# Seven products in every tile and an inverse DFT stage split by parity, in a fused spectral-filter and GELU kernel

## The chip, the cores and the metric

The kernel runs on one core of a Trainium2 chip. The metric is the device time of one launch in microseconds; the kernel before takes 768.41 us, the median of 9 runs (767.4 to 769.58).

## What is computed

```python
X = np.fft.rfft(x, axis=1)                        # x: (8, 3008, 256)
y = np.fft.irfft(X * (filt_r + 1j * filt_i), n=3008, axis=1)
h = y.reshape(24064, 256) @ w_in                  # w_in: (256, 2048)
g = 0.5 * h * (1 + erf(h / sqrt(2)))
out = g @ w_out                                   # w_out: (2048, 256)
```

Each of the 8 batches is filtered along its 3008 rows, and then 24,064 rows go through a two-layer MLP with an exact GELU. Inputs and output are float32; the products run in bfloat16 and float16.

## The kernel before, in words

**The filter.** 3008 is 47 x 64, so the transform is done as products with small matrices. `s1` (L291) is the DFT over the 47 rows that lie 64 apart; its products have 64 output rows and 47 input rows, so they use a quarter of TensorE each. Its result goes to DRAM (`R1`) and comes back as `b_sb` through `r1` (L314), turned so that the other index lies on the partitions. `s2` (L321) is the DFT over 64, for two frequencies k a step (12 steps a batch), with its twiddles in the table T2, one matrix for each of 24 k. It then multiplies by the filter: real and imaginary parts are swapped by two copies on ACT (L332, L333), and DVE takes two products and a sum (L334 to L336). `s3` (L340) is the inverse over 64, with one matrix of T3 for each k; its result goes to DRAM (`R2`) and comes back as `d_sb` through `r2` (L360). `s4` (L369) is the inverse over 47, with one small matrix T4 for all columns, and writes the filtered rows into a ring (`y_sb`) that holds two batches. The copies out of PSUM in s1, s3 and s4 are all made by DVE (`_evac`, L273).

Batch 0 has stages of its own (`c1` to `c4`), which transpose on TensorE instead of going through DRAM. Its `c2` (L409) multiplies by the filter in one DVE operation on 1024 columns (L420) and leaves the sum to the products of `c3`, with two matrices each. The filters are loaded into partitions 0 to 63 and copied to 64 to 127 (`dup_filters`, L97).

**The MLP.** The 24,064 rows are 47 tiles of 512. `mm1` (L482) makes one block of 128 hidden columns a call with two products of 512 columns (L490), and ACT's GELU takes it out of PSUM (L493). `mm2` (L495) is the second product: per slot four products of 256 columns (L517), with two copies and two stores a tile. `mm2_seven` (L563) is the same with seven half-size products instead of eight (Strassen-Winograd): per slot seven products of 128 columns (L578). It needs sums of the activations on DVE (`sums_1` to `sums_3`, L541 to L561: eight operations of 128x1024 a tile), eight DVE combinations (L591 to L601), and sums of the second weights, which POOL makes once (`weight_sums`, L527). It is used in 25 of the 47 tiles: the odd ones from 1 to 39, and 41 to 45.

**The order.** The order of every engine's instructions is the order in which the program calls them. It is written out by hand: time is cut into slots, 16 to a tile. In slot 16 t + jc the program calls what `put` has entered there, then the second product of tile t - 1, part jc, then the first product of tile t, part jc (L774 to L781). The stages of a later batch b are entered before the slot `hi` in which its first tile starts (L746 to L763): s1 from hi - 94, r1 at hi - 80, s2 from hi - 69 every 3.5 slots, each s3 four slots after its s2, r2 at hi - 24, s4 in the last 17. From slot 82 on one batch's stages begin every 96 slots. Batch 1 has its own numbers. Loads of x, of filters and of weights stand on POOL's queue; the loads of the batch after next wait there for an s2 result through a one-element copy (`gate`, L102). All other transfers, the stores of the output among them, stand on SP's queue in the order of the calls.

**Buffers.** PSUM has three banks for mm1 ("h"), two for mm2 ("o") and three for the stages ("f"); each s1 borrows one h bank. In SBUF `pa`, `pb`, `pp`, `pv` and `pd` hold the results of s1, r1, s2, s3 and r2.

Of the kernel before, what the change touches and what calls it, by code (L numbers as in the profile page):

```python
# [19 lines left out]
K1 = 24  # L20
# [10 lines left out]
class _Mix:  # L31
    def __init__(self, ctx, tc, x, filt_r, filt_i, w_in, w_out, out):
        self.tc, self.nc = tc, tc.nc
        self.x, self.filt_r, self.filt_i = x, filt_r, filt_i
        self.w_in, self.w_out, self.out = w_in, w_out, out
        self.B, self.S, self.D = x.shape
        self.DFF = w_in.shape[1]
        assert self.S == NA * NB and self.D == 256 and self.DFF == 2048
        pool = lambda name, bufs, **kw: ctx.enter_context(tc.tile_pool(name=name, bufs=bufs, **kw))
        P = bass.MemoryType.PSUM  # L40
        self.const = pool("const", 1)
        self.px = pool("px", 1)
        self.pa = pool("pa", 3)
        self.pb = pool("pb", 4)
        self.pp = pool("pp", 4)
        self.pv = pool("pv", 3)
        self.pd = pool("pd", 3)
        self.pool = pool
        self.po = pool("po", 4)
        self.py = pool("py", 1)  # L50
        self.pg = pool("pg", 2)
        self.pq = pool("pq", 1)
        self.small = pool("small", 1)
        self.dram = pool("dram", 2, space=bass.MemoryType.DRAM)
        c = self.const
        self.T1 = c.tile([2 * NA, 96], BF16, name="T1")
        self.T2 = c.tile([128, K1, 2, NB], BF16, name="T2")
        self.T3 = c.tile([128, K1, 2, NB], BF16, name="T3")
        self.T4 = c.tile([96, NA, 2], BF16, name="T4")
        self.T4c = c.tile([96, NA, 2], BF16, name="T4c")  # L60
        self.F = c.tile([128, 2, K1, 256], BF16, name="F")
        self.w_in_sb = c.tile([128, 2, self.DFF], BF16, name="w_in_sb")
        self.w_out_sb = c.tile([128, 16, self.D], FP16, name="w_out_sb")
        self.w_sums = c.tile([128, 4, 8, 128], FP16, name="w_sums")
        self.ps, self.st = {}, {}
        self.flip = 0
# [29 lines left out]

    def dup_filters(self, eng, k0, k):  # L97
        for k in range(k0, k0 + k, 2):
            o, i = (self.F[r:r + 64, :, k:k + 2, :].rearrange("p t a b -> p t (a b)") for r in (64, 0))
            (eng.copy if eng is self.nc.scalar else eng.tensor_copy)(out=o, in_=i)  # L100
# [6 lines left out]
    def load_next(self, b, p, c, h):  # L107

        self.gate(self.st[b, "p", p][0:1, 0:1])
        self.load_x(b + 1, 8 * c, 8, (h,))  # L110
# [93 lines left out]
    def weights_4(self, g):  # L204

        ts = self.nc.gpsimd.tensor_scalar
        q, self.wt = (g.tile([128, 1], FP32, name=n) for n in ("q48", "wt"))
        ts(out=q, in0=self.p, scalar1=48.0, scalar2=-48.0, op0=ALU.is_ge, op1=ALU.mult)
        self.nc.gpsimd.tensor_tensor(out=q, in0=self.p, in1=q, op=ALU.add)
        ts(out=self.wt, in0=q, scalar1=2.0, scalar2=1.0, op0=ALU.is_ge, op1=ALU.add)  # L210
# [79 lines left out]

    def s1(self, b, c):  # L291
# [13 lines left out]
        for i in range(2):  # L305
            for h in range(2):
                self._evac(a[:, h, 2 * i:2 * i + 2, :].rearrange("p a b -> p (a b)"), ps[i][h], False)
# [13 lines left out]
    def s2(self, b, p):  # L321
        nc = self.nc
        ps = self.bank("ps_s2")
        for i in range(2):
            k = 2 * p + i
            nc.tensor.matmul(ps[:, 256 * i:256 * i + 256], lhsT=self.T2[:, k].rearrange("p a b -> p (a b)"),  # L326
                             rhs=self.st[b, "b", k // 6][:, k % 6, :], start=True, stop=True)

        w = self.pp.tile([128, 2, 512], BF16, tag="p12", name="p12")
        p1, p2 = w[:, 0], w[:, 1]  # L330
        f = lambda t: self.F[:, t, 2 * p:2 * p + 2, :].rearrange("p a b -> p (a b)")
        nc.scalar.activation(out=p2[0:64], in_=ps[64:128], func=AF.Copy, scale=-1.0)  # L332
        nc.scalar.copy(out=p2[64:128], in_=ps[0:64])  # L333
        nc.vector.tensor_tensor(out=p1, in0=ps, in1=f(0), op=ALU.mult)  # L334
        nc.vector.tensor_tensor(out=p2, in0=p2, in1=f(1), op=ALU.mult)
        nc.vector.tensor_tensor(out=p1, in0=p1, in1=p2, op=ALU.add)  # L336
        self.st[b, "p", p] = p1


    def s3(self, b, p):  # L340
        nc = self.nc
        if p == 0:
            self.st[b, "R2"] = self.dram.tile([48, NB, 256], BF16, tag="R2", name="R2")
        if p % 2 == 0:
            self.st[b, "v"] = self.pv.tile([128, 4, 256], BF16, tag="v", name="v_sb")
        vt, R2 = self.st[b, "v"], self.st[b, "R2"]
        ps = self.bank("ps_s3")
        w = self.st.pop((b, "p", p))
        for i in range(2):
            k = 2 * p + i  # L350
            nc.tensor.matmul(ps[:, 256 * i:256 * i + 256], lhsT=self.T3[:, k].rearrange("p a b -> p (a b)"),  # L351
                             rhs=w[:, 256 * i:256 * i + 256], start=True, stop=True)
        i = (p % 2) * 2
        self._evac(vt[:, i:i + 2, :].rearrange("p a b -> p (a b)"), ps, False)
        if p % 2 == 1:
            k = 2 * (p - 1)
            o = R2.rearrange("(k r) n c -> (r n) k c", r=2)
            nc.sync.dma_start(out=o[:, k:k + 4, :], in_=vt)

    def r2(self, b, c):  # L360
        d = self.pd.tile([96, 8, 256], BF16, tag="d", name="d_sb")
        self.st[b, "d", c] = d
        R2 = self.st[b, "R2"]
        for g in range(2):
            n = g * HB + c * 8
            self.nc.sync.dma_start(out=d[g * 48:g * 48 + 48, :, :], in_=R2[:, n:n + 8, :])


    def s4(self, b, grp, half):  # L369
# [4 lines left out]
        t4 = self.T4.rearrange("p a b -> p (a b)")  # L374
        for i in range(4):
            nc.tensor.matmul(ps[:, 94 * i:94 * i + 94],  # L376
                             lhsT=d[:, (grp % 2) * 4 + i, 128 * half:128 * half + 128],
                             rhs=t4, start=True, stop=True)
        yv = self.ring[:, half, o:o + self.S].rearrange("c (m w) -> c m w", w=HB)[:, :, 4 * grp:4 * grp + 4]
        pv = ps[:, 0:376].rearrange("c (i m) -> c m i", i=4)  # L380
        self._evac(yv, pv, False, 1.0 / self.S)
# [233 lines left out]
def kernel(  # L615
# [29 lines left out]
    cols = m.iota(g, "cols", [128, 128], [[1, 128]])  # L645
# [11 lines left out]
    m.T3i = m.pg.tile([128, K1, 2, NB], BF16, tag="g", name="T3i")  # L657
# [6 lines left out]
    m.dup_filters(nc.gpsimd, 4, 20)  # L664
# [54 lines left out]
    m.T1p = g.tile([2 * NA, 2, K1, 2], BF16, name="T1p")  # L719
    nc.gpsimd.tensor_copy(out=m.T1p, in_=m.T1.rearrange("p (h r k) -> p h k r", h=2, r=2))  # L720
    m.table_1_tiles(g)
    m.load_x(1)
    m.load_w_out(0)
    m.load_w_out(8)
    m.weights_4(g)
# [20 lines left out]
    for b in range(1, B):  # L746
        hi = first(b)
        if b == 1:
            s1, n1, r1, s2, n2, r2, s4, n4 = 0, 4, 15, 25, 2.8, 61, 68, 0.72
        else:  # L750
            s1, n1, r1, s2, n2, r2, s4, n4 = hi - 94, 3.5, hi - 80, hi - 69, 3.5, hi - 24, hi - 17, 1
        for u in range(16):
            put(s4 + int(u * n4), m.s4, b, u // 2, u % 2)
        for c in range(4):
            put(s1 + int(c * n1), m.s1, b, c)
            put(r1, m.r1, b, c)
            put(r2, m.r2, b, c)
        for p in range(12):
            put(s2 + int(n2 * p), m.s2, b, p)
            put(s2 + int(n2 * p) + 4, m.s3, b, p)  # L760
        if b + 1 < B:
            for i in range(8):
                put(s2 + int(n2 * (i + 2)), m.load_next, b, i + 2, i // 2, i % 2)  # L763

    put(20, m.table_4, m.T4, m.T1p, m.wt, "f", "act")
    put(6, m.weight_sums)
    seven = [t for t in range(1, NT - 1) if t % 2 or t > 40]
# [45 lines left out]
```

## Time and profile before

| | before |
|---|---|
| median of 9 runs (lowest, highest) | 768.41 us (767.4, 769.58) |
| the profiled execution, and its span | 768.41 us, 766.6 us |
| TensorE clock granted | 1.00 |
| GELU on ACT (L493), busy | 438.5 us, 752 of 597 ns |
| s2's copies on ACT (L332, L333), busy | 98.4 us, 168 of about 585 ns |
| DVE copies of s1, s3, s4 (L278, L280), mean | 684, 685, 545 ns |
| DVE sums for the seven products (L548, L554, L561), mean | 684, 687, 683 ns |
| first mm1 of the first tile starts | 38.9 us |
| first mm2 of the first tile starts | 50.3 us |

The span runs from the first to the last instruction; 1.8 us of the profiled execution lie around it. In a line of the timeline stand the start in us, the length, the engine, the source line and operation, what it writes and reads, its size and how many are drawn together. Matmuls are pipelined: each is listed with about 0.17 us of latency, so that what one costs is read from its start to the next one's start. DVE operations of one queue overlap by about 0.08 us in the same way.

### The profile page before, as it was taken

The page shows a single profiled execution, that of the slowest core. Times are in us where ns is not written, and L with a number is a line of the kernel's source. Part 1 is how long each engine was busy: PE and PEld are TensorE (multiplying, and loading weights), DVE is VectorE, ACT ScalarE, POOL GpSimd, SP SyncE. Part 2 cuts the span into 40 slices and gives each one's busy share as a digit, 9 for nine tenths or more (in the row PEclk, how much of TensorE's full clock was granted, in tenths as well). Part 3 has the DMA queues.
Part 4 walks back from the last instruction along what each step waited for, and adds up shares of the span by engine and source line. Part 5 has one row for each costly group of instructions (what it writes and reads, how often), then busy time and mean ns, then how long its engine had stood idle before and what let it go on. Part 6 is the DMA issues. An engine that isn't in the chain of part 4 may idle for free.

```text
span 766.6 us, 17716 instructions
## 1 busy us (share of the span) xinstructions
PE 742.5 (97%) x7136; PEld 525.8 (69%) x7257; DVE 551.6 (72%) x1085; ACT 568.5 (74%) x978; POOL 77.9 (10%) x173
## 2 busy tenths in 40 slices
PE   7998999999999999999999999999999999999998
PEld 4846775767777677676677767667677766777776
DVE  8958887586786868768677696767967679636562
ACT  7878966888668875698756986569865798667773
POOL 7851100020000200002000120001100000000000
PEclk9999999999999999999999999999999999999999
DMA  9884644456253662635526455254552422411011
GB/s 145 147 179 116 142 124 126 139 113 146 71 141 117 120 152 63 174 89 112 143 76 179 94 99 152 68 168 100 115 144 79 144 69 84 124 42 43 29 56 57
DMA packets 87283, 85.85 MB, mean 112 GB/s; under 512 B 6688, under 2 KB 77472, under 8 KB 87200
## 3 DMA queue, kind: packets, MB, share of 16 engines
q1 hardware_dynamic: 78816, 68.70, 31.2%
q0 software_dynamic: 8384, 16.00, 14.5%
q8 instruction: 57, 0.93, 0.5%
q14 instruction: 26, 0.21, 0.1%
HBM read 54.00 MB, written 46.66 MB: 131 GB/s over the span
## 4 chain that ended last, share of the span: by engine, by line
PE 86%; DVE 6%; ACT 3%; DMA 2%; issue 2%; POOL 0%; DVEq 0%; POOLq 0%; SPq 0%
PE ps_h L490 36%; PE ps_o L517 20%; PE ps_o L578 19%; PE ps_s L376 3%; PE ps_s L351 2%; PE ps_s L326 2%; PE ps_s L303 2%; ACT g_sb L493 2%; DVE s_sb L548 1%; DVE p L334 1%; DMA R<-a_sb 1%; ACT p L332 1%; PE ps_c L438 1%; DMA x_sb<-in_x_dram 1%; DMA F<-in_filt_i_dram 1%
## 5 line engine op out<-in xcount | busy, mean ns | idle before, releaser
L493 ACT ACTIVATE g_sb<-ps_h 128x512 f16<-128x512 f32 x752 | 438.5, 597 | 177.8 <-PE ps_h L490 148.7
L490 PE MATMUL ps_h<-y_sb,w_in_sb 128*128 128x512 bf16 (+3 forms) x1483 | 420.9, 365 | 1.7 <-DVE a_sb L278 1.6
L517 PE MATMUL ps_o<-w_out_sb,g_sb 128*128 128x256 f16 x1392 | 207.3, 273 | 1.6
L517 PEld LDWEIGHTS <-g_sb 128*128 128x128 f16 x1392 | 132.9, 98 | 70.4 <-issue 9.9
L490 PEld LDWEIGHTS <-w_in_sb 128*128 128x128 bf16 x1600 | 138.1, 98 | 15.7 <-issue 2.5
L578 PEld LDWEIGHTS <-g_sb 128*128 128x128 f16 x1600 | 106.0, 98 | 43.7 <-DVE g_sb L554 6.9
L334 DVE TENSOR_TENSOR p<-ps_s,F 128x512 bf16<-128x512 f32 x84 | 57.9, 689 | 63.4 <-ACT p L333 29.6
L578 PEld LDWEIGHTS <-s_sb 128*128 128x128 f16 x1200 | 81.5, 98 | 21.4
L278 DVE CAST a_sb<-ps_s 128x512 bf16<-128x512 f32 x112 | 69.5, 684 | 28.4 <-PE ps_s L303 26.1
L280 DVE TENSOR_SCALAR y_sb<-ps_s 128x376 bf16<-128x376 f32 x112 | 58.9, 545 | 38.1 <-PE ps_s L376 37.6
L578 PE MATMUL ps_o<-w_sums,g_sb 128*128 128x128 f16 x800 | 70.5, 219 | 4.5 <-DVE g_sb L554 3.8
L578 PE MATMUL ps_o<-w_out_sb,g_sb 128*128 128x128 f16 x800 | 66.3, 219 | 3.9 <-DVE ost L523 3.2
L578 PE MATMUL ps_o<-w_sums,s_sb 128*128 128x128 f16 x800 | 69.2, 219 | 0.7
L548 DVE TENSOR_TENSOR s_sb<-g_sb 128x1024 f16<-128x1024 f16 x100 | 65.5, 684 | 2.6 <-ACT g_sb L493 2.6
L105 POOL COPY gate<-p 1x1 bf16<-1x1 bf16 x48 | 13.9, 289 | 446.5 <-DVE p L336 446.5
L278 DVE CAST v_sb<-ps_s 128x512 bf16<-128x512 f32 x84 | 57.4, 685 | 0.9 <-PE ps_s L351 0.8
L332 ACT ACTIVATE p<-ps_s 64x512 bf16<-64x512 f32 x84 | 49.9, 594 | 2.1
L333 ACT CAST p<-ps_s 64x512 bf16<-64x512 f32 x84 | 48.5, 577 | 1.0
L523 DVE COPY ost<-ps_o 128x512 f32<-128x512 f32 x43 | 29.6, 687 | 26.8 <-PE ps_o L517 26.8
L376 PEld LDWEIGHTS <-d_sb 96*128 96x128 bf16 x448 | 30.8, 97 | 25.3 <-DMA d_sb<-R 0.2
L336 DVE TENSOR_TENSOR p<-p 128x512 bf16<-128x512 bf16 x84 | 35.7, 425 | 2.9
L376 PE MATMUL ps_s<-T,d_sb 96*128 96x94 bf16 x448 | 36.3, 204 | 1.4
(131 smaller groups left out, 550.8 us busy)
## 6 DMA issues: line engine op xcount, KB each, us to landing
out_dram<-ost SPq DMA_DIRECT2D x93, 256.0 KB, 2.4
x_sb<-in_x_dram POOLq DMA_DIRECT2D x64, 188.0 KB, 3.6
R<-a_sb SPq DMA_DIRECT2D x112, 96.0 KB, 2.1
b_sb<-R SPq DMA_DIRECT2D x28, 384.0 KB, 4.6
R<-v_sb SPq DMA_DIRECT2D x42, 256.0 KB, 2.5
d_sb<-R SPq DMA_DIRECT2D x56, 192.0 KB, 4.0
w_in_sb<-in_moe_w_in_dram POOLq DMA_DIRECT2D x2, 512.0 KB, 9.9
w_out_sb<-in_moe_w_out_dram POOLq DMA_DIRECT2D x2, 512.0 KB, 12.4
```

The lines of the kernel that those rows point to most:

```text
L278: self.nc.vector.tensor_copy(out=out, in_=in_)
L280: self.nc.vector.tensor_scalar(out=out, in0=in_, scalar1=scale, scalar2=None, op0=ALU.mult)
L332: nc.scalar.activation(out=p2[0:64], in_=ps[64:128], func=AF.Copy, scale=-1.0)
L333: nc.scalar.copy(out=p2[64:128], in_=ps[0:64])
L334: nc.vector.tensor_tensor(out=p1, in0=ps, in1=f(0), op=ALU.mult)
L336: nc.vector.tensor_tensor(out=p1, in0=p1, in1=p2, op=ALU.add)
L376: nc.tensor.matmul(ps[:, 94 * i:94 * i + 94], lhsT=d[:, (grp % 2) * 4 + i, 128 * half:128 * half + 128], rhs=t4, start=True, stop=True)
L490: nc.tensor.matmul(ps[:, o:o + n], lhsT=self.w_in_sb[:, dc, jc * 128:jc * 128 + 128], rhs=self.ring[:, dc, off:off + n], start=(dc == 0), ...
L493: nc.scalar.activation(out=self.st["g", t][:, jc, :], in_=ps, func=AF.Gelu)
L517: nc.tensor.matmul(ps[:, tile_i % 2, :], lhsT=g[:, jc, tile_i * 128:tile_i * 128 + 128], rhs=self.w_out_sb[:, jc, :], start=(jc == 0), sto ...
L548: self.nc.vector.tensor_tensor(out=self.st["s", t][:, i:i + 2], in0=a, in1=b, op=ALU.subtract)
L578: nc.tensor.matmul(ps[:, (m + 1) % 2, sub, :], lhsT=a[:, i, 128 * sub:128 * sub + 128], rhs=b[:, i], start=i == 0, stop=i == 7)
```

## The change

All of it is in one edit:

- `mm2_seven` is used for tiles 1 to 45 (45 instead of 25).
- s2 ends in one DVE operation that makes both products of the spectrum, with the real and with the imaginary filter, as c2 does; the two ACT copies and the sum go.
- s3 handles eight frequencies a call (four s2 steps). The rows of the spectrum are ordered by parity, so that one 64x64 matrix pair `U` serves all k; each call is 16 products of 64 input rows, 64 output rows and 512 columns into four PSUM banks, one of them an h bank. What differs between the k moves into s4, whose table `T4a` has its own 96x94 matrix for each of 32 columns. There are three calls a batch; half of the result is taken out by `s3_out` a slot later.
- The copies of s1, s3 and s4 are shared between DVE and ACT.
- The tables T2p (T2 in the new order), U and T4a are built at the start of the first batch's work: by POOL copies and products, three products and a few copies on TensorE and ACT, and 24 POOL operations for T4a.
- The filters must be in the new order for batches 1 to 7: they are written to DRAM once and read back, k 0 to 7 before the first slot and the rest at slot 16, on SP's queue.
- The second weights are loaded between the filter copies on POOL, ahead of the last six and of the x of batch 1.
- In the slots: s2 comes in groups of four (14 slots a group, 12 in batch 1) with s3 three slots after the fourth; the last r1 and the last r2 of a batch come later than the others; batch 1 loads the next x at slot 25 without gates.
- `pb`, `pp` and `pv` have 3, 6 and 2 buffers instead of 4, 4 and 3.

```diff
+    def save_filters(self):
+        self.Fd = self.dram.tile([64, 2, K1, 256], BF16, tag="Fd", name="Fd")
+        self.nc.sync.dma_start(out=self.Fd, in_=self.F[0:64])
+
+    def load_filters_again(self, k0, k):
+        for par in range(2):
+            for r in range(2):
+                for q in range(2):
+                    o = 64 * par + 32 * r + 16 * q
+                    self.nc.sync.dma_start(out=self.F[o:o + 16, :, k0:k0 + k, :],
+                                           in_=self.Fd[32 * q + (par ^ q):32 * q + 32:2, :, k0:k0 + k, :])
...
+    def table_4_all(self, g):
+        tt = self.nc.gpsimd.tensor_tensor
+        a, b = (self.t4[:, o:o + 8 * NA].rearrange("p (w m) -> p w m", w=8) for o in (224, 608))
+        to = self.T4a.rearrange("p w (m h) -> p h w m", h=2)
+        for w in range(0, HB, 8):
+            for h in range(2):
+                n = HB * h + w
+                for o, x in ((a, 0), (b, 1)):
+                    tt(out=o, in0=self.fcs[:, n:n + 8, x:x + 1].to_broadcast([96, 8, NA]),
+                       in1=self.G[:, x].unsqueeze(1).to_broadcast([96, 8, NA]), op=ALU.mult)
+                tt(out=to[:, h, w:w + 8], in0=a, in1=b, op=ALU.add)
...
     def s1(self, b, c):
-                self._evac(a[:, h, 2 * i:2 * i + 2, :].rearrange("p a b -> p (a b)"), ps[i][h], False)
+                self._evac(a[:, h, 2 * i:2 * i + 2, :].rearrange("p a b -> p (a b)"), ps[i][h], "act" if h else False)
...
     def s2(self, b, p):
-        nc.scalar.activation(out=p2[0:64], in_=ps[64:128], func=AF.Copy, scale=-1.0)
-        nc.scalar.copy(out=p2[64:128], in_=ps[0:64])
-        nc.vector.tensor_tensor(out=p1, in0=ps, in1=f(0), op=ALU.mult)
-        nc.vector.tensor_tensor(out=p2, in0=p2, in1=f(1), op=ALU.mult)
-        nc.vector.tensor_tensor(out=p1, in0=p1, in1=p2, op=ALU.add)
+        w = self.st[b, "p", p] = self.pp.tile([128, 2, 512], BF16, tag="p12", name="p12")
+        nc.vector.tensor_tensor(out=w, in0=ps.unsqueeze(1).to_broadcast([128, 2, 512]),
+                                in1=self.F[:, :, 2 * p:2 * p + 2, :].rearrange("p t a b -> p t (a b)"), op=ALU.mult)
...
+    def s3(self, b, u):
+        ps = [[self.bank("ps_s3", "h" if i == par == 0 else "f") for par in range(2)] for i in range(2)]
         for i in range(2):
+            for t in range(2):
+                for q in range(2):
+                    for par in range(2):
+                        r = slice(64 * par, 64 * par + 64)
+                        nc.tensor.matmul(ps[i][par][64 * q:64 * q + 64, :],
+                                         lhsT=self.U[r, t].rearrange("p r w -> p (r w)"),
+                                         rhs=self.st[b, "p", 4 * u + 2 * i + q][r, t, :], start=t == 0, stop=t == 1)
+        self.st[b, "ps3"] = ps
+        self.s3_out(b, u, 0)
+
+    def s3_out(self, b, u, i):
+        for par in range(2):
+            self._evac(vt[:, 2 * par:2 * par + 2, :].rearrange("p a b -> p (a b)"), ps[par], "act" if par else False)
+        for q in range(2):
+            self.nc.sync.dma_start(out=self.st[b, "R2"][:, 4 * u + 2 * i + q], in_=vt[64 * q:64 * q + 64])
...
     def s4(self, b, grp, half):
-                             rhs=t4, start=True, stop=True)
+                             rhs=self.T4a[:, 4 * grp + i], start=True, stop=True)
-        self._evac(yv, pv, False, 1.0 / self.S)
+        self._evac(yv, pv, "act" if half else False, 1.0 / self.S)
...
-    m.dup_filters(nc.gpsimd, 4, 20)
+    m.dup_filters(nc.gpsimd, 4, 8)
+    m.load_w_out(0)
+    m.load_w_out(8)
+    m.dup_filters(nc.gpsimd, 12, 12)
+    m.save_filters()
...
-            s1, n1, r1, s2, n2, r2, s4, n4 = 0, 4, 15, 25, 2.8, 61, 68, 0.72
+            s1, n1, r1, s2, n2, group, r2, s4, n4 = 0, 4, 15, 25, 2.5, 12, 62, 68, 0.72
-            s1, n1, r1, s2, n2, r2, s4, n4 = hi - 94, 3.5, hi - 80, hi - 69, 3.5, hi - 24, hi - 17, 1
+            s1, n1, r1, s2, n2, group, r2, s4, n4 = hi - 94, 3.7, hi - 80, hi - 71, 3.4, 14, hi - 25, hi - 17, 1
+        unit = lambda p: s2 + group * (p // 4) + int(n2 * (p % 4))
...
+            put(unit(p), m.s2, b, p)
+            if p % 4 == 3:
+                put(unit(p) + 3, m.s3, b, p // 4)
+                put(unit(p) + 4, m.s3_out, b, p // 4, 1)
...
-    seven = [t for t in range(1, NT - 1) if t % 2 or t > 40]
+    seven = range(1, NT - 1)
```

## Prediction

> **What bounds the kernel now.** I read the page's busy times first, then one period of a batch, then the stretch in it where PE waits. The profiled execution has a span of 766.6 us and took 768.41 us, which is also the median of the nine runs, so every sum below starts from 768.4.
>
> ```profile
> PE 742.5 (97%) x7136; PEld 525.8 (69%) x7257; DVE 551.6 (72%) x1085; ACT 568.5 (74%) x978; POOL 77.9 (10%) x173
> ...
> PE 86%; DVE 6%; ACT 3%; DMA 2%; issue 2%; POOL 0%; DVEq 0%; POOLq 0%; SPq 0%
> ```
>
> PE is the bound: 97% busy and 86% of the chain that ended last. Time comes only from fewer PE cycles or fewer PE waits. The timeline gives the two kinds of slot, one mm1 (two products of 512 columns) and one mm2 slot:
>
> ```profile
> 439.78 0.59 PE L490 MATMUL ps_h<-y_sb,w_in_sb 128*128 128x512 bf16 x2
> 440.21 0.60 PE L517 MATMUL ps_o<-w_out_sb,g_sb 128*128 128x256 f16 x4
> 440.65 0.59 PE L490 MATMUL ps_h<-y_sb,w_in_sb 128*128 128x512 bf16 x2
> ...
> 695.77 0.59 PE L490 MATMUL ps_h<-y_sb,w_in_sb 128*128 128x512 bf16 x2
> 696.20 0.55 PE L578 MATMUL ps_o<-w_sums,s_sb 128*128 128x128 f16 x7
> 696.59 0.59 PE L490 MATMUL ps_h<-y_sb,w_in_sb 128*128 128x512 bf16 x2
> ```
>
> From start to start a plain slot takes 0.87 us (440.65 - 439.78) and a seven-product slot 0.82 (six in a row: 692.91 to 697.85, 0.823 each). I use 0.046 us as the gain of a converted slot. The next lines, from the table of stretches and the timeline, are one batch period (96 slots, six tiles), its worst stretch, and the block of s1:
>
> ```profile
> 210.69:304.27 93.58, 91.83 (x882) 65.58 (x900) 69.14 (x134) 70.07 (x121) 6.29 (x16) 1.00 0.49 119
> 254.60:268.20 13.60, 12.43 (x123) 8.53 (x125) 12.96 (x26) 11.33 (x21) 3.56 (x8) 1.00 0.51 102
> ...
> 303.67 0.59 PE L490 MATMUL ps_h<-y_sb,w_in_sb 128*128 128x512 bf16 x2
> 304.20 0.63 PE L303 MATMUL ps_s<-x_sb,T1s 47*64 47x512 bf16 x8
> 304.75 0.61 PE L517 MATMUL ps_o<-w_out_sb,g_sb 128*128 128x256 f16 x4
> ```
>
> Columns of the first two: length, then PE, PEld, DVE, ACT, POOL busy. In 254.6 to 268.2 a seven-product tile meets s2 and s3: DVE is busy 12.96 of 13.60 us and PE only 12.43. The gaps between neighbouring matmuls beyond their usual spacing add up to 1.9 us a batch, all of them there (0.66 at 260.7, 0.47 at 257.0, then smaller), so a batch is 91.7 us of work and 1.9 of waiting. The s1 block costs 0.55 us plus 0.10 by which the mm1 before it is stretched (0.53 instead of 0.43): 0.65 us for eight 64-column products of 512 columns. One after the other they would take 8 x 0.216 = 1.7, so four run at a time.
>
> [...] 0.65 less two groups at 0.216 leaves 0.22 us for entering and leaving. [...] The trace shows one direction:
>
> ```profile
> 441.48 0.69 DVE L548 TENSOR_TENSOR s_sb<-g_sb 128x1024 f16<-128x1024 f16 x1
> ...
> 441.69 0.51 POOL L105 COPY gate<-p 1x1 bf16<-1x1 bf16 x1 [2.10 <-DVE p L336]
> ```
>
> The one-element copy takes 0.51 us and ends when the DVE sum ends; beside no such sum it takes 0.18. DVE waiting for POOL is not in this trace. [...] here 128x256 takes 0.63 us from start to start (four in 2.54, L534), 2.4 ns an element.
>
> **The change, part by part.**
>
> *Seven products.* Twenty even tiles (2 to 40) change, 320 slots x 0.046 = 14.7 us less PE. DVE pays for it: from start to start 8 sums at 0.60 us and 8 combinations at about 0.35 (0.42 in the groups, less the 0.08 by which neighbours overlap), 7.6 us a tile instead of 1.2.
>
> *Inverse stage.* s3 was 24 products of 256 columns, 0.109 each, 2.6 us a batch. It becomes three blocks of 16 products on 64x64 tiles, four groups each: 0.65 + 2 x 0.235 = 1.12 us, 3.4 a batch. That is 0.8 more, 5.4 in seven batches. I assume s3 overlaps four at a time as s1 does; its limits are 0.216 and 0.25 a group, 1.08 to 1.15 a block. s1 (4 x 0.65), s2 (24 x 0.109) and s4 (64 x 0.042 = 2.7; eight of the same shape, L467, run from 33.05 to 33.39) keep their PE time.
>
> *What leaves the vector side.* In each s2 step two ACT copies (0.60 each) and three DVE operations (0.60 + 0.45 + 0.34 from start to start: 430.09, 430.69, 431.15 for the first two) become one DVE product, as in c2: nine L420 in 10.28 us, 1.14 each. Half of the copies of s1, s3 and s4 go to ACT (0.60, 0.60, 0.48), and s3's copies halve. Per batch DVE goes from 67.3 us (mixing 40.9, tiles 3 x 7.6 + 3 x 1.2) to 13.7 + 4.8 + 3.6 + 3.7 + 6 x 7.6 = 71.4, ACT from 72 to about 70, both well under 93. What counts is one group of s2 and s3, 14 slots: DVE 4 x 1.14 + 2 x 0.60 + 14/16 x 7.6 = 12.4 us, PE 14 x 0.823 + 0.87 + 1.12 = 13.5: 92%. In the worst stretch of before the demand around the tile boundary was higher (1.39 + 0.60 per 3.5 slots against 1.14 + 0.30) and ACT lay on the chain too, but now three boundaries a batch fall in this stage instead of one. At the tightest alignment (s2 of the last group one slot before a tile boundary) the sums, the four combinations and the copy of the borrowed h bank queue about 1 us behind on DVE; PE then waits for that bank or the second sum. I take 0.47 us a group, 1.4 a batch; bounds 0.1 and 1.6 a group.
>
> *Steady batch.* 96 x 0.823 = 79.0, s1 2.6, s2 2.6, s3 3.4, s4 2.7: 90.3, plus 1.4 waiting, 91.7. Against 93.6 that is -1.9, and in six periods -11.4 us.
>
> *Moved loads.* s2 now starts 12 slots after the last s1 instead of 15: 12 x 0.823 and the s1 block are 10.5 us, and the way from that s1 over R1 to the first b_sb took 9.5 (314.87 to 324.36), with two engines copying now instead of one; hidden with 1 us to spare, and what is missing PE would wait for. The fourth r1 (20 slots ahead of its use, 6.2 us to landing) and the fourth r2 (7 slots, 3.6) are issued when their smaller pools are free, so SP no longer stands before them, and s4 starts 12 slots after the last s3 copy instead of 10, room for an R2 read in 512-byte pieces instead of 4 KB ones: nothing. A converted tile's two stores both stand at its last slot instead of one in the middle; on SP they come just ahead of r1, which waits longer for R1: nothing.
>
> *First batch (slots 16 to 81, 50.3 to 117.1).* 18 slots convert (-0.8), s3 adds 0.8: nothing net. Before, its work was 63.8 us and its waiting 3.0. After: s2 and s3 come in 12-slot groups at 97% DVE, 2.3 us of waiting in all; s4 starts 8 slots (6.6 us) after the last s3 copy, and the way over R2 took 6.1 us from the end of that copy to the landing (issue 96.47, d_sb 102.57), so with 1 to 2 us for the copy PE waits about 1.0; and table_4_all puts 24 operations of 376 elements on POOL, 24 x 0.9 = 22 us, from about 54 on, beside some 12 sums of tiles 1 and 2. If the lock works both ways each sum waits 0.2 on average, 2.5 us; bounds 0 and 5. Sum 5.8 of waiting: +2.8. POOL's own lateness is hidden: T4a is needed at slot 68 (about 105 us), the x loads behind it only at slot 82.
>
> *Start.* The two w_out loads (0.93 us of POOL each) now stand before the last six filter copies; POOL waited 0.45 there, and c2 follows those copies at 1.14 each with a lead of 0.2: +1.2 us. In slots 0 to 15 eight s1 copies and four table copies (about 5 us) join 16 gelus (0.52 each) on ACT: 13.3 us where PE took 12: +0.8. For it, R1's writes no longer meet w_out (5.3 us to landing instead of about 2; PE lost 1.58 at 49.5). Saving and reloading the filters puts 1.5 MB out and 1 MB in on SP's queue ahead of R1, so I count half of that: -0.8. The other 2 MB of filters go out at slot 16, behind three r1 loads, needed 21 slots later: nothing; if late, s2 stands still. Sum +1.2, bounds -0.5 and +5.
>
> Together: 768.4 - 11.4 + 2.8 + 1.2 = 761.0 us.
>
> **The rivals.**
>
> *Hardly any new waits.* The s2 chain loses its ACT half (29.6 us of DVE waits on L333 vanish) and PE waits 0.4 a batch; the lock costs nothing. 90.7 a batch, -2.9 x 6, the rest even: 751. For it: ACT falls to 72% in the group stage.
>
> *Front end eats it.* Start +4, first batch +7: 768. For it: 97% DVE, the lock, the longer SP queue. Against: long leads on every table.
>
> *Slower: DVE becomes the bound of the group stage.* s3 needs four s2 products, stands three slots (2.5 us) after the last, and that product itself takes 1.2 plus 0.45 to get its input; if one sum and one more product stand ahead of it, PE waits about 1.6 us in each of 21 groups. A batch takes 90.3 + 4.8 = 95.1 (+1.5 x 6), the first 63.8 + 4.8 + 1.0 + 2.5 (+5.3), the start +1.2: 784. From about 0.85 us a group the change is a loss. For it: an in-order DVE at 92%. Against: most s2 steps meet a short queue.
>
> **How the numbers follow.** Forecast 761 (755 to 766) 0.57, few waits 0.17, front end 0.14, slower 0.12. The range 750.5 to 768.5 leaves out the slower case and the ends of the two others. This kernel's runs can tell about 0.2% (1.5 us): faster 0.79, same 0.09, slower 0.12.
>
> **What would show it.** Right: a batch period near 91.7 us, s3 blocks near 1.1 us, no L332 and L333, PE gaps small and at tile boundaries. Wrong: s3 products one after the other, gaps over 0.85 us at s3, DVE sums longer than 0.69 us beside POOL, s4 or the first s2 waiting for a DMA.

## The result, and the profile after

The changed kernel takes 764.19 us, the median of 10 runs (759.53 to 765.75). Beside it on the same chips the kernel before takes 768.33. The ratio is 0.9938, 95% interval 0.9926 to 0.995: faster by 0.6%. The forecast was 761.0. The profiled execution of the kernel after took 762.34 us with a span of 760.6, some 1.9 us less than its median, so it lies 6.1 us under the profiled execution of before. One execution among all that follow, of the version with the plain reload at slot 13, took 1,952 us, some 2.6 times as long as the other three of it; it is left out, and so that version has no trace.

First the busy times and the shares of the chain that ended last, from the page of the kernel after.

```profile
PE 730.9 (96%) x8253; PEld 518.4 (68%) x8388; DVE 582.6 (77%) x1043; ACT 547.6 (72%) x967; POOL 111.5 (15%) x207
...
PE 80%; DMA 6%; DVE 6%; ACT 2%; POOL 2%; issue 2%; SPq 0%; DVEq 0%; POOLq 0%; ACTq 0%
```

PE is busy 11.6 us less, but the chain now has 6% of DMA where it had 2%. Three stretches tell where the time went. I take the start of the first mm2, the start of batch 2's first s1, and the periods from one batch's first s1 to the next (five, up to batch 7's):

| | before | after | forecast of the difference | measured |
|---|---|---|---|---|
| start of the span to first mm2 | 50.33 | 58.90 | +1.2 | +8.6 |
| first batch, to batch 2's s1 | 66.77 | 69.25 | +2.8 | +2.5 |
| each later batch | 93.5 to 93.6 | 90.6 to 90.7 (one of five 91.4) | -1.9 | -2.8 on average |
| from batch 7's first s1 to the end of the execution | 183.6 | 180.3 | | -3.3 |

Five periods (-13.8), the end, the first batch and the start sum to -6.1, the difference of the two executions. In the period of 91.4 PE stands for 0.76 us ahead of s4, until a read of R2 lands. The next lines are the table of stretches of the kernel after: one steady batch, then the first batch.

```profile
128.22:218.78 90.56, 89.43 (x1022) 62.97 (x1044) 73.98 (x130) 66.94 (x118) 7.58 (x16) 1.00 0.52 123
...
58.90:128.15 69.25, 64.48 (x672) 44.64 (x682) 52.54 (x81) 45.91 (x82) 27.62 (x34) 1.00 0.72 151
```

In a steady batch PE stands for 1.1 us of 90.56 by the busy times, against 1.75 of 93.58 before; DVE is busy for 74.0 us of it, more than the 69.1 of before, and yet PE hardly waits for it. The timeline of the kernel after shows the start, where mm1 of tile 0 should have begun at 39 us:

```profile
43.78 0.60 PE L387 MATMUL ps_s<-x_sb,T1s 47*64 47x512 bf16 x1 [4.76 <-DMA x_sb<-in_x_dram]
45.70 1.07 PE L387 MATMUL ps_s<-x_sb,T1s 47*64 47x512 bf16 x7 [1.32 <-DMA x_sb<-in_x_dram]
...
46.70 1.46 PE L569 MATMUL ps_h<-y_sb,w_in_sb 128*128 128x512 bf16 x3
```

PE waits for x of batch 1: 4.76 us, and 1.32 more in the middle of the first s1 block (in square brackets: the wait and who ended it). The eight x loads landed from 43.6 to 53.3 us; before, from 32.8 to 41.5. The last part of the page gives the transfers that are new, each with its size and the median us to landing:

```profile
F<-Fd SPq DMA_DIRECT2D x8, 256.0 KB, 12.5
Fd<-F SPq DMA_DIRECT2D x1, 1536.0 KB, 11.5
```

The save of the filters was under way from 22.1 to 33.6 us, the first eight reloads (1 MB) from 33.7 to 51.3, the other eight (2 MB) from 62.2 to 83.0. So the start is the stretch that went wrong, and two things in it are suspects: w_out, which now stands ahead of x, and the filters' way out and back.

### The profile page after: what moved, and what is told of

Its sections match the earlier page's. It is cut to its first block, busy times and chain, and to the rows that moved or that the text cites. A ratio compares the mean times of both kernels' runs of the same rounds, so it can differ in the third digit from the quotient of the medians.

```text
span 760.6 us, 20047 instructions
## 1 busy us (share of the span) xinstructions
PE 730.9 (96%) x8253; PEld 518.4 (68%) x8388; DVE 582.6 (77%) x1043; ACT 547.6 (72%) x967; POOL 111.5 (15%) x207
## 4 chain that ended last, share of the span: by engine, by line
PE 80%; DMA 6%; DVE 6%; ACT 2%; POOL 2%; issue 2%; SPq 0%; DVEq 0%; POOLq 0%; ACTq 0%
PE ps_o L657 35%; PE ps_h L569 34%; PE ps_s L455 3%; DMA x_sb<-in_x_dram 3%; PE ps_s L427 2%; PE ps_s L410 2%; DVE p L413 2%; PE ps_s L387 2%; ACT g_sb L572 2%; DVE s_sb L627 2%; PE ps_o L596 1%; POOL F L113 1%; DMA out_dram<-ost 1%; DMA d_sb<-R 1%; DMA R<-v_sb 1%
## 5 line engine op out<-in xcount | busy, mean ns | idle before, releaser
L657 PEld LDWEIGHTS <-g_sb 128*128 128x128 f16 x2880 | 190.2, 98 | 80.3 <-issue 15.2
L657 PEld LDWEIGHTS <-s_sb 128*128 128x128 f16 x2160 | 147.4, 98 | 51.5 <-issue 3.3
L657 PE MATMUL ps_o<-w_sums,g_sb 128*128 128x128 f16 x1440 | 125.0, 219 | 2.1 <-DVE g_sb L633 1.3
L657 PE MATMUL ps_o<-w_sums,s_sb 128*128 128x128 f16 x1440 | 124.5, 219 | 1.1
L627 DVE TENSOR_TENSOR s_sb<-g_sb 128x1024 f16<-128x1024 f16 x180 | 120.7, 694 | 0.0
L657 PE MATMUL ps_o<-w_out_sb,g_sb 128*128 128x128 f16 x1440 | 118.4, 219 | 1.9
L413 DVE TENSOR_TENSOR p<-ps_s,F 128x1024 bf16<-128x1024 f32 x84 | 102.6, 1221 | 18.3 <-PE ps_s L410 15.6
L633 DVE TENSOR_TENSOR g_sb<-s_sb,g_sb 128x1024 f16<-128x1024 f16 x90 | 63.1, 701 | 1.1
L657 PE MATMUL ps_o<-w_out_sb,s_sb 128*128 128x128 f16 x720 | 62.2, 219 | 0.5
L640 DVE TENSOR_TENSOR s_sb<-g_sb 128x1024 f16<-128x1024 f16 x90 | 61.4, 683 | 0.0
L672 DVE TENSOR_TENSOR ost<-t_sb,ps_o 128x256 f32<-128x256 f32 x45 | 18.9, 419 | 31.2 <-PE ps_o L657 31.2
L680 DVE TENSOR_TENSOR ost<-t_sb,ps_o 128x256 f32<-128x256 f32 x90 | 33.7, 416 | 6.8 <-PE ps_o L657 6.8
## 6 DMA issues: line engine op xcount, KB each, us to landing
F<-Fd SPq DMA_DIRECT2D x8, 256.0 KB, 12.5
Fd<-F SPq DMA_DIRECT2D x1, 1536.0 KB, 11.5
```

The costliest lines, as they stand in the source:

```text
L413: nc.vector.tensor_tensor(out=w, in0=ps.unsqueeze(1).to_broadcast([128, 2, 512]), in1=self.F[:, :, 2 * p:2 * p + 2, :].rearrange("p t a b ...
L627: self.nc.vector.tensor_tensor(out=self.st["s", t][:, i:i + 2], in0=a, in1=b, op=ALU.subtract)
L633: self.nc.vector.tensor_tensor(out=a21[:, k], in0=self.st["s", t][:, k, 0], in1=a22[:, k], op=ALU.add)
L640: self.nc.vector.tensor_tensor(out=self.st["s4", t][:, k], in0=a12[:, k], in1=s2[:, k], op=ALU.subtract)
L657: nc.tensor.matmul(ps[:, (m + 1) % 2, sub, :], lhsT=a[:, i, 128 * sub:128 * sub + 128], rhs=b[:, i], start=i == 0, stop=i == 7)
L680: v(out=c(h, 1 - h), in0=tt, in1=p, op=ALU.add)
```

## The experiments

Every ratio is to the kernel before. Starts and periods are read from each run's trace.

**w_out behind x again.** Theory: w_out ahead of x delays x. Rival: the filter traffic does.

```diff
-    m.load_w_out(0)
-    m.load_w_out(8)
...
     m.load_x(1)
+    m.load_w_out(0)
+    m.load_w_out(8)
```

> Undoes one part: the two loads of the second weights stand again behind the x of batch 1 on POOL's queue; saving and reloading the filters stays. In the profile of after, s1 of batch 1 begins at 43.8 us (38.4 before) because x_sb lands only at 43.6, and the first mm2 at 58.9 instead of 50.3. Theory (x is late because w_out stands ahead of it): s1 begins before 40.5, the first mm2 before 53, total 755 to 758. Rival (x is late because the filters' 2.5 MB share the DMA engines): s1 still begins after 42, total 761 to 764.

765.3 us, 0.9959 (0.9943 to 0.9975): nothing gained over the kernel after. The first mm1 did come at 39.1, but the first mm2 only at 56.1 and batch 2 at 131.9. PE waited 4.3 us, until 52.6, for a copy that a write of R1 held up, and 4.1 us, until 87.0, for DVE, which had stood until just after the last reloaded filters landed at 83.3. The order of the loads chooses who waits; the sum of the traffic stays.

**No save and reload.** It leaves the re-order of the filters out, so that batches 1 to 7 are multiplied by filters in the old order.

```diff
-    m.save_filters()
...
-    m.load_filters_again(0, 8)
...
-    put(16, m.load_filters_again, 8, 16)
```

> Leaves out the saving of the filters to DRAM and both reloads, so that batches 1 to 7 are multiplied with filters in the old row order; w_out stays ahead of x. Theory (w_out ahead of x): w_out still has to pass first, but passes in about 7 us instead of 14, s1 begins at 39 to 41, total 757 to 760, less gain than putting w_out behind x. Rival (filter traffic): s1 begins at 38.5 to 39.5, the first mm2 before 52, total 754 to 757, more than the other edit gains.

752.08 us, 0.9794 (0.9778 to 0.9811): 11 to 12 us less than the kernel after. The periods were the same. mm1 began at 39.6 and batch 2 at 118.4. Of the first mm2 the timeline of the kernel after has

```profile
58.90 0.60 PE L596 MATMUL ps_o<-w_out_sb,g_sb 128*128 128x256 f16 x4
```

and the timeline of this run

```profile
51.12 0.60 PE L596 MATMUL ps_o<-w_out_sb,g_sb 128*128 128x256 f16 x4
```

The filter traffic is the cause, and of its price 7.8 us lie at the start and 2.0 in the first batch.

**Neither.** The same, with w_out behind x as well.

> Both edits: w_out behind x again, and no saving and no reloading of the filters (batches 1 to 7 get filters in the old row order). If the transfers are the whole of the lost start, s1 begins at about 38.4 as before, the first mm2 at 51 to 52 (0.8 us of ACT copies stay), and the total is 754 to 756. If what ACT and POOL do in slots 0 to 15 costs more than 2 us, the first mm2 stays after 53 and the total at 757 or more.

753.79 us, 0.9813 (0.9799 to 0.9828). The first mm2 comes at 51.0, against 51.1 with w_out ahead of x. The profiled execution (754.6 us), in which PE waited 2.0 us ahead of s4, had a mean clock of 0.998, and so had two others; the one of the four at a clock of 1.00 took 752.2 us, the same as the run before it. This clears w_out.

**What makes the filter traffic dear?** The reloads write 16 partitions each. The kernel after's own landings (seven of the eight of its second reload), seen one after the other while little else moved, and those of a form with 32 partitions a transfer:

```
256 KB into 16 partitions (after):   69.07 71.15 73.23 75.31 77.39 79.46 81.55   2.08 us each: 126 GB/s
512 KB into 32 partitions (below):   65.89 68.34 70.80 73.16                     2.42 us each: 216 GB/s
```

Why the narrower form moved fewer bytes a second, the traces do not show. In packets: 8 KB took about 1040 ns in the first form and about 600 in the second, and the packets' times sum to 15 under way at once in both. So the engines count as busy all the same; the table of stretches shows the DMA share (next to last column) full (1.01) at 141 GB/s (last) in the kernel after,

```profile
66.50:83.00 16.50, 15.20 (x141) 10.26 (x142) 13.66 (x14) 10.02 (x18) 15.64 (x17) 1.00 1.01 141
```

and full (1.02) at 245 GB/s in the run with s4 two slots later (below), which has the other form:

```profile
61.30:73.20 11.90, 11.86 (x110) 8.14 (x111) 10.67 (x11) 7.00 (x13) 11.35 (x12) 1.00 1.02 245
```

Two versions of a wider form came first and were far slower. Both write 64 partitions a transfer, with a leading dimension of two on the side of DRAM that reads each row twice; the save is in two writes that make the parity order. The second also moves the first reload to slot 13. The edit of the reload:

```diff
-            for r in range(2):
-                for q in range(2):
-                    o = 64 * par + 32 * r + 16 * q
-                    self.nc.sync.dma_start(out=self.F[o:o + 16, :, k0:k0 + k, :],
-                                           in_=self.Fd[32 * q + (par ^ q):32 * q + 32:2, :, k0:k0 + k, :])
+            for t in range(2):
+                a = self.Fd[32 * par:32 * par + 32, t, k0:k0 + k, :]
+                a = dataclasses.replace(a, ap=[[0, 2], [2 * K1 * 256, 32], [1, 256 * k]])
+                self.nc.sync.dma_start(out=self.F[64 * par:64 * par + 64, t, k0:k0 + k, :], in_=a)
```

> The kernel after, with the same bytes of filters moved at the same places, but the order by parity is made when they are saved (two writes of 32 partitions), so that each reload is four transfers of 64 partitions instead of eight of 16. In after a packet of 8192 bytes of the second reload took 1042 ns, 7.9 bytes a ns; packets of b_sb (3072 bytes, 128 partitions) took 144 ns, 21. Theory (the narrow form of the reload keeps the DMA engines busy): packets of 8192 bytes under 500 ns, both reloads land in under 8 us, s1 of batch 1 begins at 39 to 40.5, first mm2 at 51 to 53, total 753 to 756. Rival (the number of bytes): packets stay near 1000 ns and the total at 761 to 765.

> As the wide reload, and its first half (k 0 to 7) is issued in slot 13, behind R1's writes on SP, instead of before slot 0. Theory (narrow form): with wide transfers the place matters little, total 752 to 755, up to 1.5 us better than the wide reload at its old place. Rival (bytes): what counts is that nothing is ahead of x and R1; the total falls by 5 us or more against the wide reload at its old place.

813.26 us, 1.0575 (1.054 to 1.0609), and 812.84 us, 1.0577 (1.0553 to 1.0601). The first mm2 stood at 71.9 and 53.8 us, batch 2 at 179 in both. The answer for the tile `F` in the first of them names the wait:

```profile
its engine sat idle before it (us, times) until:
  DMA F<-Fd: 39.6, 1
  PE ps_s L413: 1.6, 2
```

Single packets were faster (8 KB in 376 ns on average), but only 1.7 of them were under way at once, and the 2 MB took from 77.2 to 133.3 us: 37 GB/s. Why so few, the trace does not show. So these two say nothing on the first question.

**The plain form.** The parity order is made while saving, in 4 writes, and each reload is 4 transfers of 32 partitions.

```diff
-        self.nc.sync.dma_start(out=self.Fd, in_=self.F[0:64])
+        for q in range(2):
+            for e in range(2):
+                o = 32 * (e ^ q) + 16 * q
+                self.nc.sync.dma_start(out=self.Fd[o:o + 16], in_=self.F[32 * q + e:32 * q + 32:2])
...
-                for q in range(2):
-                    o = 64 * par + 32 * r + 16 * q
-                    self.nc.sync.dma_start(out=self.F[o:o + 16, :, k0:k0 + k, :],
-                                           in_=self.Fd[32 * q + (par ^ q):32 * q + 32:2, :, k0:k0 + k, :])
+                o = 64 * par + 32 * r
+                self.nc.sync.dma_start(out=self.F[o:o + 32, :, k0:k0 + k, :],
+                                       in_=self.Fd[32 * par:32 * par + 32, :, k0:k0 + k, :])
```

> Same bytes and same places as in the changed kernel, other form: the parity order is made while saving (4 writes of 16 partitions), and each reload is 4 plain transfers of 32 partitions. If the form of the reload (8 transfers of 16 partitions out of every second row, 8 KB pieces in 1.04 us each) is what costs, pieces of the reload take about half, mm2 starts near 53 to 55 us, batch 2's s1 near 121, the total 753 to 758. If the bytes on the shared DMA engines are what costs, all stays as in the changed kernel: 761 to 765. The 7.9 and 20 bytes per ns of the two forms leave both open.

759.31 us, 0.9875 (0.9834 to 0.9916). The second reload went at the higher rate, but in the profiled execution (762.8 us) PE still waited 5.9 us for x and mm2 began at 58.8: x and the first reload meet all the same. Two executions had granted clocks of 0.993 and 0.990 and took 762.8 and 762.1 us, two had 1.00 and 0.998 and took 756.2 and 756.5. In the profiled one the wait for x was followed by a clock of 0.50 (in all stretches from 42 to 48 us), so the wait was probably shorter in the two at 1.00 and 0.998, but no trace shows it. The form alone is part of an answer.

**The first reload later as well.**

```diff
-    m.load_filters_again(0, 8)
...
+    put(13, m.load_filters_again, 0, 8)
```

> As the run before it, and k 0 to 7 are read back at slot 13 instead of ahead of the first slot, so that x of batch 1 and w_out meet only the save. If form and place both count: mm1 of tile 0 starts near 41 us, mm2 near 53, total 752 to 755, the best version that computes all. If only the form counts, no difference from the run before it. If only the bytes count, the first batch takes what the start gains, total 760 or more.

0.9825 (0.9801 to 0.9848), 753.1, 753.7 and 756.4 us: together with the next version the best that computes all. Form and place both count, as the first of the three theories had it. For the form the intervals are apart (0.9926 to 0.995 in the kernel after). For the place they overlap by a little, and the trace of the next version has to carry it: mm2 at 52.8 instead of 58.8. The old form at slot 13 was not run, and the two forms differ not only in partitions but also in the rows that they read (every second one, or all), so the share of each is not known.

**s4 of batch 1 two slots later.** Built on that version, it also gives the profile of the start for both.

```diff
-            s1, n1, r1, s2, n2, group, r2, s4, n4 = 0, 4, 15, 25, 2.5, 12, 62, 68, 0.72
+            s1, n1, r1, s2, n2, group, r2, s4, n4 = 0, 4, 15, 25, 2.5, 12, 62, 70, 0.65
```

> As the version that reads k 0 to 7 back at slot 13 in plain transfers, and s4 of batch 1 stands in slots 70 to 79 instead of 68 to 78. The way over R2 was costed at about 1.0 us of waiting; PE waited 1.6 to 2.0 us ahead of the first s4 in the runs with a clean start. If that wait is the way over R2, two slots (1.65 us) take up all but some tenths of it, and the total is 752 to 753 against 753.7. If it comes from the queue of copies on DVE and ACT, a tighter s4 makes it longer: no gain, 754 or more. The start should show mm1 of tile 0 near 41 us and mm2 near 53, since this run also has the profile of the start that the late, plain reload gives.

754.33 us, 0.9828 (0.9815 to 0.9841): no gain. mm1 began at 41.3 and mm2 at 52.8, as expected, but PE still waited ahead of the first s4:

```profile
107.95 0.51 PE L457 MATMUL ps_s<-T4a,d_sb 96*128 96x94 bf16 x8 [1.45 <-DMA d_sb<-R]
```

The two first reads of R2 were issued at 102.45 us and landed 4.5 and 5.0 us later, where without the filter traffic the same two took 3.1 and 3.6. It is the way over R2, not the copies, but that way is not a fixed length: two slots (1.65 us) were given and some 1.4 us of them were taken by slower reads. Why these were slower stays open.

**The lock between DVE and POOL.** The question is whether each holds the other up. Read against the run without save and reload. It leaves out that re-order and the 24 POOL operations that make s4's table.

```diff
-        for w in range(0, HB, 8):
+        self.nc.gpsimd.memset(self.T4a, 0.5)
+        for w in ():
```

> Without the re-order of the filters and without the 24 GpSimd operations that make the table of s4 (one fill with a constant in their place, so s4's table and the filters of batches 1 to 7 are wrong). It is to be read against the run without the re-order of the filters, whose first batch took 67.3 us (51.1 to 118.4) at 752.1 us. If the lock between DVE sums and GpSimd costs PE time as I put it in the sum, the first batch takes 64.6 to 65.5 us and the total is 749.5 to 750.5. If the lock is hidden, 67 us or more, and the same total.

750.93 us, 0.978 (0.9765 to 0.9794). The first batch took 65.5 us instead of 67.3, the table of stretches of this run:

```profile
51.23:116.73 65.50, 64.03 (x687) 44.66 (x685) 49.65 (x81) 45.92 (x83) 7.11 (x10) 1.00 0.51 130
```

and that of the run without save and reload:

```profile
51.12:118.41 67.29, 63.75 (x672) 44.62 (x681) 52.38 (x81) 45.92 (x82) 28.09 (x33) 1.00 0.50 124
```

DVE is busy 2.7 us less for the same 81 operations, and the batch is 1.8 us shorter. Gone with the table are PE's waits of 0.72 and 0.42 us for DVE at 72.2 and 73.2 us, and 0.36 us of its wait ahead of s4. In the timeline of the kernel after, the sums stand beside the table's operations like this:

```profile
72.97 0.97 POOL L373 TENSOR_TENSOR T4a<-t_sb 96x376 bf16<-96x376 f32 x1
73.26 1.23 DVE L627 TENSOR_TENSOR s_sb<-g_sb 128x1024 f16<-128x1024 f16 x1
...
76.03 0.98 POOL L373 TENSOR_TENSOR T4a<-t_sb 96x376 bf16<-96x376 f32 x1
76.14 1.42 DVE L633 TENSOR_TENSOR g_sb<-s_sb,g_sb 128x1024 f16<-128x1024 f16 x1
```

and in the timeline of the run without the table:

```profile
67.72 0.68 DVE L634 TENSOR_TENSOR g_sb<-s_sb,g_sb 128x1024 f16<-128x1024 f16 x1
68.32 0.68 DVE L628 TENSOR_TENSOR s_sb<-g_sb 128x1024 f16<-128x1024 f16 x1
```

The two sums of the kernel after began while a POOL operation ran and ended 0.55 us after its end: 1.23 and 1.42 us instead of 0.68. In the run without save and reload five sums of the first batch took 1.20 to 1.43 us, all others 0.67 to 0.69. With the POOL copy that the prediction showed (0.51 us instead of 0.18), each of the two engines was held up beside the other. The totals of the two runs have intervals that overlap, so the 1.8 us rest on the traces.

**Which part of the change brings the steady gain?** Three runs. Seven products only in the tiles that had them:

```diff
-    seven = range(1, NT - 1)
+    seven = [t for t in range(1, NT - 1) if t % 2 or t > 40]
```

> The kernel after, with seven products only in the tiles of before (odd tiles up to 39, and 41 to 45): the new inverse stage alone. Theory (steady batches: 90.3 us of PE work plus 0.3 of waits): 48 slots are 0.046 us longer, so a batch period of 92.5 to 93.0, and the total about 14 us over that of after less what the lock and the DVE queue cost in the first batch, 774 to 777. Rival (the inverse stage itself brings the steady gain): period under 92, total under 770.

774.69 us, 1.0088 (1.0063 to 1.0113); periods 92.58 and 92.64. Beside before (93.55) the inverse stage, with all else that changed, gains 0.95 a batch although its blocks cost PE 0.6 more (3 x 1.08 us for 24 x 0.109); beside the kernel after (90.6) the sevens gain 2.0.

Seven products in all tiles of the kernel before, with its old inverse stage:

```diff
-    seven = [t for t in range(1, NT - 1) if t % 2 or t > 40]
+    seven = range(1, NT - 1)
```

> The kernel before with seven products in tiles 1 to 45 and nothing else: the old inverse stage stays. PE work per batch 91.7 - 2.2 = 89.5, 0.8 less than in after. DVE 40.9 + 45.6 = 86.5 us a batch, and with the tile boundary in the s2 stage three times a batch, each costing about 1.9 us as before: period 95 or a little more, total 772 to 780 (theory: the new inverse stage is what makes the seven products pay). Rival (the seven products pay by themselves): period 91 to 92, total 755 to 760, better than after.

802.99 us, 1.046 (1.0427 to 1.0493), worse than any theory here had it. Periods are 98.8 to 99.4, and PE's longest waits by what ended them were all for DVE, which was busy 87.4 us of 99.0:

```profile
PE ps_o L578 <- DVE ost L601: 19.4, 25, 2.1
PE ps_o L578 <- DVE g_sb L554: 16.5, 20, 1.0
PE ps_s L351 <- DVE p L336: 8.5, 12, 0.8
```

All copies of s1, s3 and s4 on DVE, in the kernel after (the edit is the same in all three; s3's is shown):

```diff
-            self._evac(vt[:, 2 * par:2 * par + 2, :].rearrange("p a b -> p (a b)"), ps[par], "act" if par else False)
+            self._evac(vt[:, 2 * par:2 * par + 2, :].rearrange("p a b -> p (a b)"), ps[par], False)
```

> The kernel after with all copies of s1, s3 and s4 on DVE again. DVE gets 8 x 0.60 + 6 x 0.60 + 8 x 0.46 = 12.1 us more a batch, 86 of 90.6. Theory (the steady waits vanished because every stage leaves DVE some slack): the group stage is at 14 x 0.823 + 2 = 13.5 us of PE against 13.6 of DVE and begins to wait; period 91.5 to 93.5, total 768 to 778. Rival (the end of the ACT half of the s2 chain is what removed the waits, DVE has slack enough): period under 91, total within 2 us of after.

779.31 us, 1.0145 (1.0118 to 1.0173); periods 92.3 to 93.6. PE's waits for DVE in it, the second of them for the combination that frees an mm2 bank:

```profile
PE ps_s L410 <- DVE v_sb L297: 5.8, 7, 2.7
...
PE ps_o L657 <- DVE ost L680: 4.0, 6, 0.8
```

Some 5 us of the 16 between the two profiles are not these: the first mm2 came 2.6 us later, after 8.8 us of waiting for x, and the first batch took 2.1 us longer.

So neither half of the change stands alone: the sevens need room on DVE, and the inverse stage without the sevens does not earn its start. That the shared copies make part of this room is shown; what the one-operation s2 makes of it no run separates.

## Why the prediction was right, and where it was wrong

The sign and the range held, with luck. The forecast gain was 7.4 us; by the medians it is 4.1, by the two profiles 6.1. The sum came this close because two wrong terms stood against each other: the start was put 7.4 us too low (+1.2 for +8.6), and the six later batches gained 5.7 us more than forecast (-17.1, end included, for -11.4).

*Start: wrong, a term mis-sized.* The step was "Saving and reloading the filters puts 1.5 MB out and 1 MB in on SP's queue ahead of R1, so I count half of that: -0.8". It was counted as the loss of half of a gain, 0.8 us; by the run without it, it costs 7.8 us before the first mm2. I looked at the order in SP's queue only. But x and w_out stand on POOL's queue and share the DMA engines, and these were already full there, at a share of 1.14. The table of stretches of the kernel before has, with the DMA share next to last:

```profile
33.00:42.00 9.00, 8.84 (x131) 6.26 (x131) 8.67 (x15) 7.59 (x18) 2.90 (x6) 1.00 1.14 190
```

The 1.5 MB went out at 137 GB/s and the 1 MB came in at 60, 29 us in all up to 51.3, where x was wanted at 39. The 126 GB/s measured above for 16 partitions give an estimate of 8.3 us for the 1 MB alone. The w_out term (+1.2) was nothing: without filter traffic the first mm2 comes within 0.2 us in both orders. The rival "front end eats it" had the right place and, with +4, still half the size; its +7 for the first batch was too much.

*A second price of the same wait.* The wait of 4.76 us was followed by half the clock. Of the kernel after, in stretches of 2 us (the third number from the end is the clock):

```profile
38.00:40.00 2.00, 0.91 (x18) 0.61 (x14) 1.44 (x3) 1.55 (x5) 0.00 (x0) 1.00 1.15 217
40.00:42.00 2.00, 0.00 (x0) 0.00 (x0) 0.00 (x0) 0.00 (x0) 0.17 (x1) 1.00 1.25 164
42.00:44.00 2.00, 0.22 (x1) 0.16 (x2) 0.00 (x0) 0.00 (x0) 1.96 (x4) 0.51 1.07 197
44.00:46.00 2.00, 0.68 (x5) 0.18 (x6) 0.00 (x0) 0.00 (x0) 1.89 (x4) 0.50 1.15 178
46.00:48.00 2.00, 2.00 (x10) 0.48 (x5) 1.29 (x2) 1.25 (x3) 1.90 (x9) 0.50 1.29 164
48.00:50.00 2.00, 1.78 (x13) 0.65 (x12) 0.00 (x0) 1.76 (x4) 1.60 (x7) 0.78 1.05 180
```

PE stood from 39.0 to 43.8, the clock was 0.50 from 42.06 to 48.88, and products of mm1 came 0.43 us apart instead of 0.22. In the run with s4 two slots later, where PE waited 1.4 us for x and not 4.8, the clock stayed at 1.00. It cost about 0.7 us here: first mm1 to first mm2 took 12.2 us, against 11.5 there. Shorter waits differ: the run with neither, with 2.0 us ahead of s4, had a mean clock of 0.998 over its 752.7 us (an estimate of some 3 us, if it was at half), and the run without save and reload, with 1.8 us there, one of 1.00. Seven of the ten executions of the kernel after had a mean clock of 0.993, the profiled one 0.996; so most probably lost more to this than the trace shows.

*The second reload: wrong, and smaller.* "Needed 21 slots later: nothing" failed on the need itself: 21 slots are 17 us, and the last of the eight transfers landed 20.9 us after the first was issued, at 83.03 us. s2's fifth step, the first that uses them, stood until then:

```profile
83.41 1.23 DVE L413 TENSOR_TENSOR p<-ps_s,F 128x1024 bf16<-128x1024 f32 x1 [1.85 <-DMA out_dram<-ost]
```

The profile names a store, but the two stores under way landed only at 84.4 and 85.0, so I take it to be the filters. In the run with w_out behind x the same operation waited 5.5 us, until 83.65, with the last transfer landed at 83.28. Without the filter traffic it did not wait. PE then stood 0.76 us at the next s3 block and 0.57 for a sum. The rest of the queue was late too (two stores landed after 15.2 and 9.9 us, the fourth b_sb after 10.4), but I see no wait for it. With the rest of the filter traffic it is worth 2.0 us of the first batch.

*First batch: right in sum, other parts.* Forecast waits 5.8 over a floor of 63.8. The clean runs give the parts: without re-order and table 65.5, of which 64.0 are work and 1.5 a wait ahead of s4 (forecast 1.0), with no wait in the groups (forecast 2.3); the lock 1.8 (forecast 2.5, as 0.2 for each of some 12 sums; it was about 0.6 for each of five); the filter traffic 2.0 (forecast nothing).

*Steady batch: the floor right, the waits mis-sized.* Forecast 90.3 and 1.4 of waiting; measured 90.6. The spacing of PE's products in the batch from 128 us shows one gap, of 0.16 us at 157.8, in a seven-product slot, as a combination on DVE ends. DVE at 92% of a group (in the trace 12.5 of 13.0 us from 153 to 166) did not become a queue in front of PE: this was the rival with few waits, which I gave 0.17. s3 went as assumed, four products at a time: four start within 0.01 us, and the next four 0.22 to 0.24 us after the first. In the line

```profile
174.94 1.06 PE L427 MATMUL ps_s<-p,U 64*64 64x512 bf16 x16
```

the length has the latency in it; from start to start a block takes 0.99 us and stretches the mm1 before it by 0.09, 1.08 for the 1.12 of the forecast. Entering and leaving cost 0.09 each of this: 0.31 us from the product before to the block's first and from its last to the next product, instead of 0.22. The rival in which DVE becomes the bound did not come about in the kernel after; the old inverse stage with sevens everywhere shows that it was real. Two of the prediction's signs of being wrong did appear, DVE sums longer than 0.69 us beside POOL and s4 waiting for a DMA, at about the prices that it had put on them.

## What to carry to other kernels

Price a transfer that is added to a stretch with full DMA engines by its bytes over the rate of its own form, whatever queue it stands on: here it was paid by whichever other load was needed first. Transfers of 16 partitions were slow here (126 GB/s) and kept the engines busy all the same; making the order while saving and reading back 32 partitions at a time was better (216 GB/s). When an engine is near its bound in a stage, test the room before counting on either part of a change that makes and uses it.

## What the runs showed that I had not expected

- After 4.8 us of waiting PE's clock was 0.50 for 6.8 us. With a wait of 2.0 us one run had a mean clock of 0.998, with one of 1.8 us another had 1.00.
- Of equal bytes and with some 15 packets under way at once in both, 16 partitions a transfer moved 126 GB/s and 32 moved 216.
- The transfers with a leading dimension of two had 1.7 packets under way at once and moved 37 GB/s.
- A DVE sum beside a POOL operation of 0.98 us took up to 1.42 us instead of 0.68, and POOL's own stretched as well (up to 1.27 for a product of 0.82).
- Entering and leaving the 64x64 products of s3 cost PE 92 ns each.
